# Loading the second pair ahead of theta's weight, with the first batch's orders rewritten on every engine

## The chip, the cores and the metric

The program runs on one core of one Trainium2 chip. The metric is device time of one execution in microseconds (us), lower is better. All times are medians over several executions; every execution quoted here was in the normal ("fast") state, so like is compared with like. "The clock" below is the granted TensorE clock that the profile records, as a share of full speed (1.00). In the views of the profile PE is TensorE (matrix products), PEld its weight loads, DVE VectorE, ACT ScalarE, POOL GpSimd and SPq the queue that issues transfers (DMA); L312 is line 312 of the kernel shown.

## The reference, cut to what matters

Two stages in sequence. The first is retention (linear attention with decay) over 4 batches, 8 heads, 768 steps and 64 elements a head; the second takes its output as `x` (4 x 768 x 512).

```python
# stage 1, per batch and head
state = gamma * state + outer(k[t], v[t])
y[t]  = scale * q[t] @ state
# stage 2
theta = x @ w_theta
zr, zi = x * cos(theta), x * sin(theta)
y = w_tok_r @ zr + w_tok_i @ zi          # mixes the 768 steps
u = x + y
out = u + maximum(u @ w_ch, 0)
```

Everything arrives as float32; the kernel computes its products in bfloat16.

## The kernel before

A batch is cut into three "pairs" of 256 steps (pair `n`, each with two halves of 128), so there are 12 pairs; pairs 0 to 2 are the first batch. For each pair the kernel does:

- `prep`: cast k, scale q and v by the decay (out of the float32 tile `pair`), `flip`: transpose k and q on TensorE and copy the result out of its PSUM tile (`kqT<-kq_ps` in the views, 0.69 us on VectorE);
- `ret_A` score block, `ret_mask` its mask on VectorE, `ret_S` state, `ret_Y` output within the block, `ret_I` output from the earlier state ("inter-chunk block"), `ret_out` copy to `xT`;
- `x_pe`: transpose `xT` back to `x`; `theta`: four matmuls and two sines on ScalarE; `zmul`: the two products `z` on VectorE;
- `moe_M`: the token mix, one step being two matmuls (it needs the transposed token weights, `w_flip`, and one z), then `moe_u`, `moe_U`, `moe_O`, `moe_out` and the store.

With `tc.manual_schedule()` the order of the lines in this source is the schedule of every engine at once. The first batch is a hand-written list before the main loop, cut here to the part that the argument touches:

```python
loads("p0 th p1 w0 p2 w1 w2 p3 w3 ch p4 w4 p5 w5")   # order of the DMA loads
def keep_busy(times):                                # filler, computes nothing wanted
    for _ in range(times):
        nc.tensor.matmul(warm_ps, warm[:, 0:P], warm, start=True, stop=True)
DP, PP = (DV, PL), (PL, PL)       # halves of a scaling: VectorE + GpSimd, or GpSimd alone
...                               # pair 0: prep, flips, retention
theta(0, 0); flip(1, "k"); theta(0, 1); flip(1, "q")
prep(1, "v", PP); w_cast(0); x_pe(0, None)
ret_A(1, 0); ret_mask(1, 0)
...                               # rest of pair 1
prep(2, "k", (PL,)); zmul(0, 0); flip(2, "k"); prep(2, "q", DP)
theta(1, 0); zmul(0, 1); theta(1, 1)
moe_M(0, 0, 1)
flip(2, "q"); prep(2, "v", PP); w_cast(1); w_cast(2); x_pe(1, AC.copy)
moe_M(0, 1, 2)
ret_A(2, 0); ret_mask(2, 0); ret_S(2, 0); state_out(2, 0)
ret_A(2, 1); ret_mask(2, 1); zmul(1, 0)
...
for n in range(nG, B * nG + 1):   # main loop from pair 3 on; round n starts retention of pair n
    ...
```

Of the kernel before, what the change touches and what calls it, by code (L numbers as in the profile page):

```python
# [14 lines left out]
FT = mybir.dt.float32  # L15
# [17 lines left out]
def kernel(  # L33
# [64 lines left out]
    def loads(order):  # L98
        for what in order.split():
            if what == "th":  # L100
                load_w512("th", moe_w_theta)
            elif what == "ch":
                load_w512("ch", moe_w_ch)
            elif what[0] == "w":
                for r in range(2):
                    load_wtok(r, int(what[1:]))
            else:
                for name in "kqv":
                    load(int(what[1:]), name)

    loads("p0 th p1 w0 p2 w1 w2 p3 w3 ch p4 w4 p5 w5")


    warm = const.tile([P, dm], BF)
# [72 lines left out]
            copy(t, ps)  # L187
        st[n, name + "T"], st[n, name + "_ps"] = t, ps

    def flip_out(n, name):  # L190
        nc.vector.tensor_copy(st[n, name + "T"], st[n, name + "_ps"])

    def flip_dma(n, name):
        t = work.tile([P, 2, NP, P], BF, name="kqT", bufs=6)
# [112 lines left out]
             st[n, "x_ps"].rearrange("p a j e -> p a (j e)"))  # L307

    def theta(n, a):
        th_ps = psum.tile([P, dm], FT, name="th_ps", tag="acc", bufs=2)  # L310
        for j in range(NP):
            nc.tensor.matmul(th_ps, st[n, "xT"][:, a, j, :], wth[:, j, :], start=(j == 0),  # L312
                             stop=(j == NP - 1))
        cs = work.tile([P, 2, dm], BF, name="cs", bufs=3)
        nc.scalar.activation(cs[:, 0, :], th_ps, AF.Sin, bias=halfpi, scale=1.0)  # L315
        nc.scalar.activation(cs[:, 1, :], th_ps, AF.Sin, bias=zerob, scale=1.0)  # L316
        st[n, "cs", a] = cs
# [53 lines left out]

    def moe_out(m):
        b, t0 = divmod(m, nT)
        ot = work.tile([P, dm], FT, name="ot", bufs=8)
        nc.vector.scalar_tensor_tensor(ot, mo[m]["o"], 0.0, mo[m]["u"], ALU.max, ALU.add)  # L375
        mo[m]["ot"] = ot

# [3 lines left out]

    wrow = {}

    def w_cast(t0):
        for r in range(2):
            row = work.tile([P, S], BF, name="wrow", bufs=5)
            nc.gpsimd.tensor_copy(row, wdma[r, t0])  # L387
            wrow[r, t0] = row

    def w_flip(r, t0, copy=True):  # L390
# [71 lines left out]
    def keep_busy(times):  # L462
        for _ in range(times):
            nc.tensor.matmul(warm_ps, warm[:, 0:P], warm, start=True, stop=True)
# [10 lines left out]
    flip(0, "q")  # L475
    keep_busy(2)
    prep(0, "v", PP)
    nc.gpsimd.tensor_copy(wth, wdma["th"])
    ret_A(0, 0)
    ret_mask(0, 0)  # L480
    keep_busy(2)
    ret_S(0, 0)
    state_out(0, 0)
    ret_A(0, 1)
    ret_mask(0, 1)
    ret_Y(0, 0)
    keep_busy(1)
    ret_S(0, 1)
    ret_I(0, 1)
    state_out(0, 1)  # L490
    prep(1, "k", (AC,))
    keep_busy(1)
    ret_Y(0, 1)
    ret_out(0, 0, DV.tensor_copy)
    ret_out(0, 1, DV.tensor_copy)
    keep_busy(3)
    prep(1, "q", DP)
    theta(0, 0)
    flip(1, "k")
    theta(0, 1)  # L500
    flip(1, "q")
    prep(1, "v", PP)
    w_cast(0)
    x_pe(0, None)
    ret_A(1, 0)
    ret_mask(1, 0)
    x_out(0, DV.tensor_copy)
    keep_busy(3)
    ret_S(1, 0)
    state_out(1, 0)  # L510
    ret_A(1, 1)
    ret_mask(1, 1)
    ret_Y(1, 0)
    ret_I(1, 0)
    w_flip(0, 0)
    ret_S(1, 1)
    state_out(1, 1)
    ret_I(1, 1)
    ret_Y(1, 1)
    ret_out(1, 0, AC.copy)  # L520
    ret_out(1, 1, DV.tensor_copy)
    w_flip(1, 0)
    prep(2, "k", (PL,))
    zmul(0, 0)
    flip(2, "k")
    prep(2, "q", DP)
    theta(1, 0)
    zmul(0, 1)
    theta(1, 1)
    moe_M(0, 0, 1)  # L530
    flip(2, "q")
    prep(2, "v", PP)
    w_cast(1)
    w_cast(2)
    x_pe(1, AC.copy)
    moe_M(0, 1, 2)
    ret_A(2, 0)
    ret_mask(2, 0)
    ret_S(2, 0)
    state_out(2, 0)  # L540
    ret_A(2, 1)
    ret_mask(2, 1)
    zmul(1, 0)
    ret_Y(2, 0)
    ret_I(2, 0)
    ret_I(2, 1)
    w_flip(0, 1, False)
    w_flip(1, 1, False)
    ret_Y(2, 1)
    ret_out(2, 0, AC.copy)  # L550
    ret_out(2, 1, DV.tensor_copy)
    w_out(0, 1)
    w_out(1, 1)
    zmul(1, 1)
    prep(3, "k", (PL,))
    moe_M(0, 2, 3)
    theta(2, 0)
    flip(3, "k")
    prep(3, "q", DP)
    theta(2, 1)  # L560
    moe_M(0, 3, 4)
    x_pe(2)
    w_flip(0, 2, False)
    w_out(0, 2, AC.copy)
    moe_M(1, 0, 2)
    zmul(2, 0)
    flip(3, "q")
    prep(3, "v", PP)
    w_cast(3)
    moe_M(1, 2, 4)  # L570
    zmul(2, 1)
    moe_M(0, 4, 5)


    tiles_of = {nG - 2: [], nG - 1: [0, 1]}
# [16 lines left out]
    for n in range(nG, B * nG + 1):  # L592
        mine, done = tiles_of[n], tiles_of[n - 1]
        late, two = n > nG, len(mine) > 1
        nxt = n + 1 in pairs

        if nxt and n + 1 >= K_DMA:
            flip_dma(n + 1, "k")
        if nxt and n + 1 >= Q_DMA:
            flip_dma(n + 1, "q")  # L600
        if n <= X_DMA and n + 3 in pairs:
            load(n + 3, "k")
        if n >= U_DMA:
            moe_U_dma(done[1])
        def preps(engines):
            prep(n + 1, "q", engines)
            prep(n + 1, "v", PP)
            if n in (nG, nG + 1):
                w_cast(n - nG + 4)

        if n == nG:
            nc.gpsimd.tensor_copy(wch, wdma["ch"])
        if nG + 3 < n + 1 < Q_DMA:
            preps(PP)
        if late:
            ret_I(n - 1, 1)

        if n in pairs:
            ret_A(n, 0)
            ret_mask(n, 0)  # L620
        if n == nG:
            moe_M(0, 5, nT)
            w_flip(1, 2)
            moe_u(0)
            moe_M(1, 4, nT)
            moe_u(1)
        if late:
            ret_Y(n - 1, 1)
            ret_S(n - 1, 1)
            ret_out(n - 1, 0, nc.scalar.copy)  # L630
            ret_out(n - 1, 1, nc.scalar.copy)
            state_out(n - 1, 1)
            if n < nG + 3:
                prep(n + 1, "k", (PL,))
                if n > nG + 1:
                    preps(DP)
            if n - 1 >= X_DMA:
                x_dma(n - 1)
        if n > X_DMA and n + 3 in pairs:
            load(n + 3, "k")  # L640
        if n + 3 in pairs:
            load(n + 3, "q")

        first = mine[0]
        moe_M(first, 0, 3 if two else 2)
        if late:
            theta(n - 1, 0)
            if n - 1 < X_DMA:
                x_pe(n - 1)
            if n == nG + 1:  # L650
                preps(DP)
            theta(n - 1, 1)
        if two:
            moe_M(first, 3, nT)
            moe_u(first)
        for name, limit in (("k", K_DMA), ("q", Q_DMA)):
            if nxt and nG + 1 < n + 1 < limit and (n > nG + 1 or name == "k"):
                flip(n + 1, name)
        if n + 1 >= K_DMA and not two:
            moe_M(first, 2, 4)  # L660
        if n + 3 in pairs:
            load(n + 3, "v")
        for t in stores_in(n):
            store(t)
        if n + 1 >= U_DMA:
            moe_U_dma(first)

        if n in pairs:
            ret_S(n, 0)
            state_out(n, 0)  # L670
            ret_A(n, 1)
            ret_mask(n, 1)
            ret_Y(n, 0)
            ret_I(n, 0)
        if n < U_DMA:
            moe_U(done)
        if n == nG:
            prep(n + 1, "k", (AC,))
            preps(DP)
        if n == nG or n + 1 < K_DMA and not two:  # L680
            moe_M(first, 2, 4)
        early_z = late and n < nG + 3
        if early_z and n > nG + 1:
            zmul(n - 1, 0)
        if n < nG + 3:
            w_tok(n - nG + 3)
        if early_z:
            zmul(n - 1, 0 if n == nG + 1 else 1)
        if not two:
            moe_M(first, 4, nT)  # L690
            if n == nG + 1:
                flip(n + 1, "q")
            moe_u(first)
            if n == nG + 1:
                zmul(n - 1, 1)
        elif n in pairs:
            moe_M(mine[1], 0, nT)
        if n + 2 in pairs and n > nG + 1:
            prep(n + 2, "k", (AC,))
        if n + 2 in pairs and n + 2 >= Q_DMA:  # L700
            prep(n + 2, "q", PP)
            prep(n + 2, "v", PP)
        if two and n in pairs:
            moe_u(mine[1])
        for i, t in enumerate(done):
            if n == nG:
                flip(n + 1, "kq"[i])
            moe_O(t)
            moe_out(t)
        if late and not early_z:  # L710
            zmul(n - 1, 0)
            zmul(n - 1, 1)
        if n not in pairs:
            moe_M(mine[1], 0, nT)
            moe_u(mine[1])
# [43 lines left out]
```

## Time and profile before

| what | value |
|---|---|
| median of 3 executions | 168.18 us (167.8 to 168.19) |
| TensorE busy, whole span | 93% of 166.5 us |
| granted clock | 1.00 throughout |
| first score block of pairs 0, 1, 2 | 9.90, 18.34, 27.38 us |
| theta of pair 2 begins | 32.15 us |
| inter-chunk block of pair 3 begins | 48.41 us |
| theta of pair 5 begins | 70.61 us |

The last rows are landmarks read from TensorE's timeline. The next view gives the busy time of the engines in three stretches of 10 us of the kernel before; after the stretch and its length come TensorE, weight loads, VectorE, ScalarE and GpSimd (count of instructions in brackets), then the granted clock, the DMA share and GB/s.

```profile
10.00:20.00 10.00, 8.54 (x171) 5.33 (x174) 6.93 (x9) 5.07 (x10) 7.19 (x6) 1.00 1.15 319
20.00:30.00 10.00, 8.57 (x189) 6.08 (x190) 8.69 (x12) 6.90 (x13) 7.78 (x9) 1.00 1.12 332
30.00:40.00 10.00, 9.38 (x111) 5.97 (x111) 8.86 (x13) 5.01 (x8) 7.65 (x7) 1.00 1.03 316
```

TensorE and VectorE are both close to full from 20 to 40 us: 8.57 and 9.38 us of each 10 on TensorE, 8.69 and 8.86 on VectorE.

### The profile page before, as it was taken

To read this page: it belongs to the slowest core of one execution; us is meant where nothing else is said; L and a number is where in the kernel's file an instruction comes from. 1 tells how busy PE (TensorE), PEld (TensorE's weight loads), DVE (VectorE), ACT (ScalarE), POOL (GpSimd) and SP (SyncE) were. 2 spreads that over 40 slices of the span, in tenths; PEclk is the share of its full clock that TensorE was granted. 3 is DMA by queue.
4 is the path that set the end of the run, shared out by engine and by line. 5 is a ranking of instruction groups with operands and counts; after the bars stand their busy time and mean duration, and the time that the engine had idled before them with its cause. 6 is when DMAs were issued, how large, how long until landed. Compare 5 with 4: busy or idle time off the path is not lost.

```text
span 166.5 us, 4614 instructions
## 1 busy us (share of the span) xinstructions
PE 155.2 (93%) x1933; PEld 87.2 (52%) x1959; DVE 102.4 (61%) x137; ACT 79.1 (48%) x137; POOL 66.6 (40%) x82
## 2 busy tenths in 40 slices
PE   6969897899999999999999999999999999999991
PEld 2345664664755667555555554455545444444460
DVE  2257798878686699939446464584554736334442
ACT  7216568371819467687847827447083350000010
POOL 6275959786685877771442703600000000000000
PEclk9999999999999999999999999999999999999999
DMA  4999999999999999999999999998996161753343
GB/s 122 309 345 307 326 326 354 286 328 317 293 311 349 277 278 331 309 202 250 206 231 298 163 242 203 195 233 168 266 145 185 32 189 32 231 115 100 106 141 135
DMA packets 68901, 38.45 MB, mean 231 GB/s; under 512 B 26256, under 2 KB 63376, under 8 KB 68880
## 3 DMA queue, kind: packets, MB, share of 16 engines
q1 hardware_dynamic: 68736, 38.02, 90.2%
q8 instruction: 15, 0.25, 0.7%
q10 hardware_dynamic: 144, 0.13, 0.2%
q14 instruction: 6, 0.05, 0.1%
HBM read 25.69 MB, written 6.29 MB: 192 GB/s over the span
## 4 chain that ended last, share of the span: by engine, by line
PE 77%; DVE 12%; DMA 3%; issue 3%; ACT 1%; POOL 1%; DVEq 0%; SPq 0%; POOLq 0%
PE y_ps L340 33%; PE o_ps L368 12%; PE th_ps L312 11%; PE at_ps L208 4%; PE yT_ps L231 4%; DVE at L215 4%; DMA pair<-in_q_dram 3%; PE yT_ps L245 3%; PE st_ps L262 3%; PE kq_ps L183 3%; DVE z L322 2%; PE w_ps L393 2%; DVE kqT L187 2%; PE y_ps L420 2%; DVE kqb L175 1%
## 5 line engine op out<-in xcount | busy, mean ns | idle before, releaser
L340 PE MATMUL y_ps<-z,wtr 128*128 128x512 bf16 x133 | 50.5, 379 | 1.1
L340 PE MATMUL y_ps<-z,wti 128*128 128x512 bf16 x122 | 46.2, 379 | 0.4 <-issue 0.2
L347 DVE TENSOR_TENSOR u<-y_ps,x_sb 128x512 bf16<-128x512 f32 x23 | 15.9, 690 | 27.0 <-PE y_ps L340 27.0
L215 DVE TENSOR_TENSOR at<-at_ps,maskp 128x1024 bf16<-128x1024 f32 x24 | 29.3, 1221 | 4.6 <-PE at_ps L208 4.6
L175 POOL TENSOR_TENSOR kqb<-pair,qscp 128x512 bf16<-128x512 f32 x17 | 19.3, 1150 | 28.9 <-DMA pair<-in_q_dram 26.0
L175 POOL TENSOR_TENSOR kqb<-pair,vscp 128x512 bf16<-128x512 f32 x24 | 26.6, 1131 | 5.0 <-DMA pair<-in_v_dram 4.9
L285 ACT CAST xT<-yT_ps 128x512 bf16<-128x512 f32 x20 | 13.5, 739 | 30.0 <-PE yT_ps L231 29.9
L375 DVE SCALAR_TENSOR_TENSOR ot<-o_ps,u 128x512 f32<-128x512 f32 x23 | 15.9, 690 | 13.2 <-PE o_ps L368 13.2
L312 PE MATMUL th_ps<-wth,xT 128*128 128x512 bf16 x93 | 23.2, 379 | 0.5 <-ACT xT L285 0.3
L368 PE MATMUL o_ps<-wch,uT 128*128 128x512 bf16 x92 | 22.8, 379 | 0.3
L340 PEld LDWEIGHTS <-wtr 128*128 128x128 bf16 x138 | 13.5, 98 | 13.8
L276 ACT CAST stbd<-st_ps 64x256 bf16<-64x256 f32 x40 | 14.7, 368 | 12.5 <-PE st_ps L262 12.0
L340 PEld LDWEIGHTS <-wti 128*128 128x128 bf16 x138 | 13.5, 98 | 13.6 <-ACT wti L400 0.4
L315 ACT ACTIVATE cs<-th_ps,halfpi 128x512 bf16<-128x512 f32 x24 | 16.5, 689 | 7.0 <-PE th_ps L312 6.6
L322 DVE TENSOR_TENSOR z<-cs,x_sb 128x1024 bf16<-128x1024 bf16 x24 | 18.8, 808 | 0.1
L316 ACT ACTIVATE cs<-th_ps,zerob 128x512 bf16<-128x512 f32 x24 | 16.5, 687 | 0.0
L312 PEld LDWEIGHTS <-xT 128*128 128x128 bf16 x96 | 8.9, 98 | 11.0 <-ACT xT L285 1.0
L368 PEld LDWEIGHTS <-uT 128*128 128x128 bf16 x92 | 8.8, 98 | 10.5 <-issue 0.6
L208 PE MATMUL at_ps<-kqT 64*64 64x128 bf16 x384 | 10.6, 221 | 2.6 <-DVE at L215 1.8
L430 ACT COPY uT<-u_ps 128x384 bf16<-128x384 bf16 (+1 forms) x2 | 0.7, 372 | 25.5 <-PE u_ps L429 25.5
L187 DVE COPY kqT<-kq_ps 128x1024 bf16<-128x1024 bf16 x14 | 9.6, 688 | 4.2 <-PE kq_ps L183 4.1
L387 POOL CAST wrow<-wtok 128x768 bf16<-128x768 f32 x12 | 10.5, 902 | 0.3 <-DMA wtok<-in_moe_w_tok_i_dram 0.2
(61 smaller groups left out, 164.4 us busy)
## 6 DMA issues: line engine op xcount, KB each, us to landing
pair<-in_k_dram SPq DMA_DIRECT2D x12, 512.0 KB, 6.7
pair<-in_q_dram SPq DMA_DIRECT2D x12, 512.0 KB, 7.7
pair<-in_v_dram SPq DMA_DIRECT2D x12, 512.0 KB, 8.2
out_dram<-ot SPq DMA_DIRECT2D x23, 256.0 KB, 2.6
wtok<-in_moe_w_tok_r_dram SPq DMA_DIRECT2D x6, 384.0 KB, 6.4
wtok<-in_moe_w_tok_i_dram SPq DMA_DIRECT2D x6, 384.0 KB, 5.8
w<-in_moe_w_theta_dram SPq DMA_DIRECT2D x1, 1024.0 KB, 8.3
w<-in_moe_w_ch_dram SPq DMA_DIRECT2D x1, 1024.0 KB, 8.5
```

Of the source, the lines that this page charges most:

```text
L175: engines[two].tensor_mul(dst[:, two], src[:, two], _bcast_last(sc[:, 2 * g + two], D))
L208: nc.tensor.matmul(at_ps[half, par, j, :], kT[rows, two, j, half], qT[rows, :, j, half], start=(j == 0), stop=(j == NP - 1), skip_group_ch ...
L215: nc.vector.tensor_mul(at.rearrange("p a j t -> p (a j) t"), at_ps.rearrange("p a j t -> p (a j) t"), _bcast_mid(maskp[:, two].rearrange(" ...
L276: nc.scalar.copy(stbd[(c + 1) % 2][sl, :, sl], st_ps[b][sl])
L312: nc.tensor.matmul(th_ps, st[n, "xT"][:, a, j, :], wth[:, j, :], start=(j == 0), stop=(j == NP - 1))
L315: nc.scalar.activation(cs[:, 0, :], th_ps, AF.Sin, bias=halfpi, scale=1.0)
L316: nc.scalar.activation(cs[:, 1, :], th_ps, AF.Sin, bias=zerob, scale=1.0)
L322: nc.vector.tensor_mul(zs[b][:, c], st[n, "cs", a], _bcast_mid(xs[b][:, c, :], 2))
L340: nc.tensor.matmul(y_ps, wT[r][:, s0, t0 * P:(t0 + 1) * P], zs[b][:, s0, r, :], start=(s0 == 0 and r == 0), stop=(s0 == nT - 1 and r == 1))
L347: nc.vector.tensor_add(u, mo[m]["y"], xs[b][:, t0, :])
L368: nc.tensor.matmul(o_ps, mo[m]["uT"][:, j, :], wch[:, j, :], start=(j == 0), stop=(j == nD - 1))
L375: nc.vector.scalar_tensor_tensor(ot, mo[m]["o"], 0.0, mo[m]["u"], ALU.max, ALU.add)
```

## The change

The intent: have q, k and v of the second pair at hand about 3 us sooner, so that the retention of two pairs runs without holes first and their thetas follow once theta's weight has come. For that the first batch's order is rewritten on all engines, three fillers go (27 to 24), the first rounds of the loop are rearranged, and the output tile gets 5 buffers for 8. The diff, cut to its core (lines that were only moved away are mostly left out):

```diff
-    loads("p0 th p1 w0 p2 w1 w2 p3 w3 ch p4 w4 p5 w5")
+    loads("p0 p1 th w0 p2 w1 w2 p3 w3 ch p4 w4 p5 w5")
...
-        cs = work.tile([P, 2, dm], BF, name="cs", bufs=3)
+        cs = work.tile([P, 2, dm], BF, name="cs", bufs=4)
...
-        ot = work.tile([P, dm], FT, name="ot", bufs=8)
+        ot = work.tile([P, dm], FT, name="ot", bufs=5)
...
-    theta(0, 0)
-    flip(1, "k")
-    theta(0, 1)
     flip(1, "q")
     prep(1, "v", PP)
-    w_cast(0)
-    x_pe(0, None)
+    for a in range(2):
+        nc.gpsimd.tensor_copy(wth[:, 2 * a:2 * a + 2], wdma["th"][:, 2 * a:2 * a + 2])
+    keep_busy(2)
     ret_A(1, 0)
     ret_mask(1, 0)
...
+    theta_mm(0, 0, "y")
     ret_Y(1, 1)
     ret_out(1, 0, AC.copy)
     ret_out(1, 1, DV.tensor_copy)
+    sines(0, 0)
+    w_cast(0)
+    x_pe(1)
+    theta(0, 1)
+    zmul(0, 0)
+    theta(1, 0)
+    w_flip(0, 0, False)
+    w_flip(1, 0, False)
+    w_out(0, 0)
+    w_out(1, 0, DV.tensor_copy)
+    theta(1, 1)
     prep(2, "k", (PL,))
+    zmul(0, 1)
+    moe_M(0, 0, 1)
+    flip(2, "k", None)
     prep(2, "q", DP)
+    moe_M(0, 1, 2)
+    flip_out(2, "k")
     flip(2, "q")
     prep(2, "v", PP)
+    zmul(1, 0)
+    moe_M(0, 2, 3)
     ret_A(2, 0)
     ret_mask(2, 0)
...                 # (rest of the first batch, and in the loop, round of pair 3:)
         if n == nG:
             prep(n + 1, "k", (AC,))
-            preps(DP)
+            moe_M(first, 3, nT)
+            moe_u(first)
+            w_tok(n - nG + 3)
...
-            if n == nG:
-                flip(n + 1, "kq"[i])
+            if n == nG and i == 1:
+                flip(n + 1, "k", nc.scalar.copy)
+                preps(DP)
+                flip(n + 1, "q")
             moe_O(t)
             moe_out(t)
+        if n == nG:
+            moe_M(first + 1, 0, 2)
```

More of the change, by code (lines that the diff above doesn't have):

```diff
@@ L188, in flip, with flip_out @@
         st[n, name + "T"], st[n, name + "_ps"] = t, ps
-    def flip_out(n, name):
-        nc.vector.tensor_copy(st[n, name + "T"], st[n, name + "_ps"])
+    def flip_out(n, name, copy=nc.vector.tensor_copy):
+        copy(st[n, name + "T"], st[n, name + "_ps"])
     def flip_dma(n, name):
@@ L309, in theta, with theta_mm @@
     def theta(n, a):
-        th_ps = psum.tile([P, dm], FT, name="th_ps", tag="acc", bufs=2)
+        theta_mm(n, a)
+        sines(n, a)
+    def theta_mm(n, a, tag="acc"):
+        th_ps = psum.tile([P, dm], FT, name="th_ps" if tag == "acc" else "y_ps", tag=tag,
+                          bufs=2 if tag == "acc" else 1)
         for j in range(NP):
@@ L313, in theta, with sines @@
                              stop=(j == NP - 1))
-        cs = work.tile([P, 2, dm], BF, name="cs", bufs=3)
+        st[n, "th", a] = th_ps
+    def sines(n, a):
+        th_ps = st[n, "th", a]
+        cs = work.tile([P, 2, dm], BF, name="cs", bufs=4)
         nc.scalar.activation(cs[:, 0, :], th_ps, AF.Sin, bias=halfpi, scale=1.0)
@@ L382, with w_cast @@
     wrow = {}
-    def w_cast(t0):
+    def w_cast(t0, copy=nc.gpsimd.tensor_copy):
         for r in range(2):
             row = work.tile([P, S], BF, name="wrow", bufs=5)
-            nc.gpsimd.tensor_copy(row, wdma[r, t0])
+            copy(row, wdma[r, t0])
             wrow[r, t0] = row
@@ L477 @@
     prep(0, "v", PP)
-    nc.gpsimd.tensor_copy(wth, wdma["th"])
     ret_A(0, 0)
@@ L481 @@
     keep_busy(2)
+    prep(1, "k", (AC,))
     ret_S(0, 0)
@@ L486 @@
     ret_Y(0, 0)
-    keep_busy(1)
+    flip(1, "k", AC.copy)
+    prep(1, "q", DP)
     ret_S(0, 1)
@@ L490 @@
     state_out(0, 1)
-    prep(1, "k", (AC,))
     keep_busy(1)
     ret_Y(0, 1)
-    ret_out(0, 0, DV.tensor_copy)
+    ret_out(0, 0, AC.copy)
     ret_out(0, 1, DV.tensor_copy)
-    keep_busy(3)
-    prep(1, "q", DP)
-    theta(0, 0)
-    flip(1, "k")
-    theta(0, 1)
+    keep_busy(1)
     flip(1, "q")
     prep(1, "v", PP)
-    w_cast(0)
-    x_pe(0, None)
+    for a in range(2):
+        nc.gpsimd.tensor_copy(wth[:, 2 * a:2 * a + 2], wdma["th"][:, 2 * a:2 * a + 2])
+    keep_busy(2)
     ret_A(1, 0)
     ret_mask(1, 0)
-    x_out(0, DV.tensor_copy)
-    keep_busy(3)
+    x_pe(0, None)
+    keep_busy(1)
     ret_S(1, 0)
     state_out(1, 0)
+    x_out(0, AC.copy)
     ret_A(1, 1)
@@ L514 @@
     ret_I(1, 0)
-    w_flip(0, 0)
     ret_S(1, 1)
@@ L521 @@
     ret_out(1, 1, DV.tensor_copy)
-    w_flip(1, 0)
+    sines(0, 0)
[9 more added lines that the diff above has]
+    theta(1, 1)
     prep(2, "k", (PL,))
-    zmul(0, 0)
-    flip(2, "k")
+    zmul(0, 1)
+    moe_M(0, 0, 1)
+    flip(2, "k", None)
     prep(2, "q", DP)
-    theta(1, 0)
-    zmul(0, 1)
-    theta(1, 1)
-    moe_M(0, 0, 1)
+    moe_M(0, 1, 2)
+    flip_out(2, "k")
     flip(2, "q")
     prep(2, "v", PP)
-    w_cast(1)
-    w_cast(2)
-    x_pe(1, AC.copy)
-    moe_M(0, 1, 2)
+    zmul(1, 0)
+    moe_M(0, 2, 3)
     ret_A(2, 0)
@@ L541 @@
     ret_A(2, 1)
+    zmul(1, 1)
     ret_mask(2, 1)
-    zmul(1, 0)
     ret_Y(2, 0)
@@ L546 @@
     ret_I(2, 1)
-    w_flip(0, 1, False)
-    w_flip(1, 1, False)
+    w_cast(1)
+    moe_M(0, 3, 4)
     ret_Y(2, 1)
-    ret_out(2, 0, AC.copy)
-    ret_out(2, 1, DV.tensor_copy)
-    w_out(0, 1)
-    w_out(1, 1)
-    zmul(1, 1)
-    prep(3, "k", (PL,))
-    moe_M(0, 2, 3)
-    theta(2, 0)
-    flip(3, "k")
-    prep(3, "q", DP)
-    theta(2, 1)
-    moe_M(0, 3, 4)
-    x_pe(2)
-    w_flip(0, 2, False)
-    w_out(0, 2, AC.copy)
+    ret_out(2, 0, DV.tensor_copy)
+    ret_out(2, 1, AC.copy)
+    w_flip(0, 1)
+    w_flip(1, 1)
+    theta(2, 0)
+    theta(2, 1)
+    x_pe(2)
+    prep(3, "k", (PL,))
     moe_M(1, 0, 2)
     zmul(2, 0)
+    flip(3, "k")
+    prep(3, "q", PP)
+    moe_M(1, 2, 4)
+    zmul(2, 1)
+    w_cast(2, AC.copy)
+    moe_M(0, 4, nT)
     flip(3, "q")
     prep(3, "v", PP)
-    w_cast(3)
-    moe_M(1, 2, 4)
-    zmul(2, 1)
-    moe_M(0, 4, 5)
+    moe_u(0)
+    moe_M(1, 4, nT)
+    w_flip(0, 2)
+    w_flip(1, 2)
+    moe_u(1)
     tiles_of = {nG - 2: [], nG - 1: [0, 1]}
@@ L611 @@
         if n == nG:
+            w_cast(n - nG + 3)
             nc.gpsimd.tensor_copy(wch, wdma["ch"])
@@ L620 @@
             ret_mask(n, 0)
-        if n == nG:
-            moe_M(0, 5, nT)
-            w_flip(1, 2)
-            moe_u(0)
-            moe_M(1, 4, nT)
-            moe_u(1)
         if late:
@@ L644 @@
         first = mine[0]
-        moe_M(first, 0, 3 if two else 2)
+        if n == nG + 1:
+            moe_M(first, 2, 4)
+        else:
+            moe_M(first, 0, 3 if two or n == nG else 2)
         if late:
@@ L678 @@
             prep(n + 1, "k", (AC,))
-            preps(DP)
-        if n == nG or n + 1 < K_DMA and not two:
+            moe_M(first, 3, nT)
+            moe_u(first)
+            w_tok(n - nG + 3)
+        elif n == nG + 2:
             moe_M(first, 2, 4)
@@ L684 @@
             zmul(n - 1, 0)
-        if n < nG + 3:
+        if nG < n < nG + 3:
             w_tok(n - nG + 3)
@@ L688 @@
             zmul(n - 1, 0 if n == nG + 1 else 1)
-        if not two:
+        if late and not two:
             moe_M(first, 4, nT)
@@ L695 @@
                 zmul(n - 1, 1)
-        elif n in pairs:
+        elif two and n in pairs:
             moe_M(mine[1], 0, nT)
@@ L705 @@
         for i, t in enumerate(done):
-            if n == nG:
-                flip(n + 1, "kq"[i])
+            if n == nG and i == 1:
+                flip(n + 1, "k", nc.scalar.copy)
+                preps(DP)
+                flip(n + 1, "q")
             moe_O(t)
             moe_out(t)
+        if n == nG:
+            moe_M(first + 1, 0, 2)
         if late and not early_z:
```

## The prediction

> **What bounds the kernel now.** I read the page from the top (busy time, slices), then the chain that ended last, then the timelines of TensorE, VectorE and GpSimd up to 50 us, because the change rewrites only that stretch.
>
> ```profile
> PE 155.2 (93%) x1933; PEld 87.2 (52%) x1959; DVE 102.4 (61%) x137; ACT 79.1 (48%) x137; POOL 66.6 (40%) x82
> ...
> PE   6969897899999999999999999999999999999991
> ...
> DMA  4999999999999999999999999998996161753343
> ...
> PE 77%; DVE 12%; DMA 3%; issue 3%; ACT 1%; POOL 1%; DVEq 0%; SPq 0%; POOLq 0%
> ```
>
> The reader is to see that TensorE is the bound: full from slice 9 (about 33 us) to the end, 77% of the chain. A slice is 4.16 us; only the first eight have holes, and DMA is full there too, so early on TensorE waits for data and for small chains through the other engines. Only those holes can be won. The timeline of TensorE shows them (start, duration, what):
>
> ```profile
> 9.90 0.42 PE L208 MATMUL at_ps<-kqT 64*64 64x128 bf16 x16 [0.35 <-DVE kqT L187]
> ...
> 13.88 0.82 PE L464 MATMUL y_ps<-warm 128*128 128x512 bf16 x3
> 14.77 1.04 PE L312 MATMUL th_ps<-wth,xT 128*128 128x512 bf16 x4
> ...
> 18.34 0.42 PE L208 MATMUL at_ps<-kqT 64*64 64x128 bf16 x16 [0.34 <-DVE kqT L187]
> 18.69 0.82 PE L464 MATMUL y_ps<-warm 128*128 128x512 bf16 x3
> ...
> 27.38 0.42 PE L208 MATMUL at_ps<-kqT 64*64 64x128 bf16 x16
> ...
> 29.12 0.42 PE L208 MATMUL at_ps<-kqT 64*64 64x128 bf16 x16 [1.07 <-DVE at L215]
> ...
> 32.15 1.04 PE L312 MATMUL th_ps<-wth,xT 128*128 128x512 bf16 x4 [0.32 <-ACT xT L285]
> ```
>
> These are retention of pair 0 (9.90), theta of pair 0 (14.77), retention of pairs 1 (18.34) and 2 (27.38), theta of pair 2 (32.15). L464 is filler (keep_busy) that computes nothing wanted. Issue-to-issue steps of the same timeline give the real work: four 128x512 matmuls 0.865 us, eight 128x128 transposes 0.45, six 0.335, a score block (L208) 0.3, a state block (L262) 0.3, an output block (L231) 0.36, an inter-chunk block (L245) 0.22, one step of the token mix (two matmuls) 0.43.
>
> Between 9.90 and 32.15 (22.25 us) the real work is: 4 flips of k and q 1.8, 2 of x 0.9, 4 of token weights 1.34, 4 thetas 3.46, 3 mix steps 1.3, 6 score blocks 1.8, 5 state 1.5, 6 output 2.15, 5 inter-chunk 1.1: 15.35 us. So 6.9 us are lost, of which 10 fillers are 2.16. From 32.15 to 48.41, where the inter-chunk block of pair 3 begins, the same sum gives about 15.3 us of 16.26: 1 us lost. In each of the next two loop rounds (48.41, 58.63, 68.83) about 0.5 us is lost. All that this change could win is a part of some 9 us.
>
> The second limit is the arrival of data, seen on GpSimd:
>
> ```profile
> 8.83 2.04 POOL L175 TENSOR_TENSOR kqb<-pair,vscp 128x512 bf16<-128x512 f32 x2 [0.16 <-DMA pair<-in_v_dram]
> 11.59 1.89 POOL L478 CAST wth<-w 128x2048 bf16<-128x2048 f32 x1 [0.71 <-DMA w<-in_moe_w_theta_dram]
> 15.24 1.55 POOL L175 TENSOR_TENSOR kqb<-pair,qscp 128x512 bf16<-128x512 f32 x1 [1.76 <-DMA pair<-in_q_dram]
> ...
> 23.67 1.04 POOL L175 TENSOR_TENSOR kqb<-pair,qscp 128x512 bf16<-128x512 f32 x1 [0.77 <-DMA pair<-in_q_dram]
> 25.14 2.49 POOL L175 TENSOR_TENSOR kqb<-pair,vscp 128x512 bf16<-128x512 f32 x2 [0.42 <-DMA pair<-in_v_dram]
> ```
>
> v of pair 0 is there at 8.8, theta's weight at 11.6, q of pair 1 at 15.2, q of pair 2 at 23.7 us.
>
> [...] at 29.12 TensorE idles 1.07 us behind one masked block, though other work follows in its order. So here every order is a bet on arrival times. [...] the product z (L322) takes 0.67 us at 23.14 with GpSimd idle, 1.54 at 25.19 beside the v scaling of 25.14:
>
> ```profile
> 23.14 0.67 DVE L322 TENSOR_TENSOR z<-cs,x_sb 128x1024 bf16<-128x1024 bf16 x1
> 23.73 0.68 DVE L187 COPY kqT<-kq_ps 128x1024 bf16<-128x1024 bf16 x1
> 24.33 0.93 DVE L175 TENSOR_TENSOR kqb<-pair,qscp 128x512 bf16<-128x512 f32 x1
> 25.19 1.54 DVE L322 TENSOR_TENSOR z<-cs,x_sb 128x1024 bf16<-128x1024 bf16 x1
> 26.65 0.68 DVE L187 COPY kqT<-kq_ps 128x1024 bf16<-128x1024 bf16 x1
> ```
>
> **The change, part by part.**
>
> Loads. Pair 1 (1.57 MB) goes ahead of theta's weight (1.05 MB). The bytes up to both are the same, so from the first token weights on nothing arrives sooner or later. From the 1.7 us of one k, q or v: k of pair 1 at about 10.4, q 12.2, v 14.0, theta's weight 16.7 us. Pair 1 is about 3 us earlier, theta's weight 5 us later.
>
> 9.9 to 20 us. ScalarE casts k of pair 1 at 10.4 to 11.5 and copies its flip (1.0 us) at 13.0; VectorE scales half of q at 13.5 to 14.1 and evacuates one block to 14.8; the q flip on TensorE is at 14.2, its copy 14.8 to 15.5. So pair 1's first score block is at 15.5, not 18.34: 2.8 us won. Then the chain score, mask (1.24), score, mask runs to 18.9. Theta's weight is cast in halves by GpSimd at 16.7 to 18.6, so theta of the first half of pair 0 lies at 18.6 to 19.5, just as the last mask is ready; the last output block ends at 19.9 against 22.4 before. But before had by then both thetas of pair 0 and one weight flip (2.07 us of work), and here one theta (0.87). Of 2.5 us won 1.2 are owed: 1.3 net.
>
> 20 to 33 us. The next flip of x needs the xT evacuation of ScalarE (20.0 to 20.7): 0.8 us of TensorE idle, gone from the 1.3. From there VectorE leads. It has, in its order: x copy, z, two token-weight copies (one of them ScalarE's before), z, q scaling, two flip copies, z. At 0.6 us each for copies and scaling, 0.47 for the weight copies, 0.6 for a free z and 1.5 for one that meets GpSimd (casting k at 21.9, scaling q at 23.7, v from 25.1; I take two of three as meeting), this is 4 x 0.6 + 2 x 0.47 + 0.8 + 2 x 1.5 = 7.1 us from 21.2: 28.3. The third mix step waits for that last z and stands ahead of pair 2's first score block, which so starts at about 28.3 to 28.7 instead of 27.38. Score, mask, z, mask, evacuation put theta of pair 2 at about 32.9 instead of 32.15, with one mix step (0.43) more done: 0.3 us behind, or level.
>
> 33 to 50 us. The order takes mix steps of both first tiles and both flips ahead of the loop, the third token-weight cast goes from GpSimd to ScalarE, and two mix steps of the fourth tile (0.86) are drawn into the first round. Work up to the inter-chunk block of pair 3: 15.7 us against 15.3, with 0.86 more done. Here I see one new wait: the q flip of pair 4 stands right after its k flip and needs VectorE's scaling, which is behind the evacuation of the first output: 0.6 + 0.6 us, less 0.45 of the k flip, about 0.7. On the other side the old waits here (1 us) may go.
>
> Three fillers fewer (27 to 24) take 0.65 us of TensorE time, but only where no wait replaces them; they are in the sums above. Output tiles with 5 buffers for 8: tile 8 reuses the buffer of tile 3, whose store is issued at 107.23 us and lands 2.6 us later, while its evacuation stood at 108.07. That is about 1.5 us on VectorE, which is 55% busy there, and the next block that needs it (mask of pair 10's second score block) has more slack. I count 0.
>
> Sum of my walk: 0 to +1 us. A walk by hand finds every wait that an error of 0.3 us makes, and an order that was tuned on traces has fewer; I take off about 1.2 us. That is a choice, not a reading. Prediction: 167.6 us, 0.6 below the median of 168.18.
>
> **Rivals.** (1) VectorE becomes the bound of 20 to 33 us: already 8.7 and 8.9 of each 10 us there. For it: the sums above, each z beside GpSimd. Against it: three evacuations go to ScalarE, two come back. It would make 169 to 170. (2) The order works as meant and the early hole closes: with theta and x of both pairs at hand at 20 us, TensorE's free work (4.5 us, then pair 2) runs without a hole to theta of pair 2 at about 31 us with one mix step more: 1.6 us, with the round after it 2.5: 165.7. (3) The gain is hidden by arrival: pair 2 comes no sooner than 23.67, so a win before it turns into a wait for it: 168. (4) Fewer output buffers stall the tail: 168.5 to 169.5.
>
> **Range and chances.** 2% is 3.4 us, half of all the loss before 32 us; even rival 2 does not reach it: 0.06. Slower by 2% needs VectorE to hold up TensorE by 3.4 us net: 0.03. Within: 0.91. Range 165.7 to 169.4.
>
> **What would show it.** Right: pair 1's first score block near 15.5; theta's cast waiting for DMA at 16.7; TensorE waiting for ScalarE's evacuation near 20; pair 2's first score block behind 27.4 with a wait on z; from 75 us the same sequence as before, shifted by one constant. Wrong: score blocks of pair 2 near 26 us, or z never beside GpSimd (rival 2); waits above 1 us after 107 us (rival 4); pair 1 not earlier (then the loads are not served in order).

## The result, and the profile after

The changed kernel takes 176.55 us (175.84 to 176.88, four executions) where the kernel before takes 168.19 (167.8 to 168.29, four executions). The ratio is 1.0496 (95% interval 1.046 to 1.0532): 8.3 us slower by the means. Ratios here are the mean time of one kernel's fast runs over that of the other's of the same rounds, so not quite the ratio of the quoted medians.

The page of the kernel after shows where to look: busy time, TensorE's 40 slices with the granted clock in the same slices, and the chain's shares. A slice is 4.38 us here.

```profile
PE 156.7 (89%) x1928; PEld 88.0 (50%) x1956; DVE 102.0 (58%) x135; ACT 81.7 (47%) x140; POOL 65.0 (37%) x82
...
PE   7878694787986989999999999999999999999991
...
PEclk9999998589999999999999999999999999999999
...
PE 72%; DVE 9%; DMA 5%; SPq 4%; issue 3%; ACT 2%; POOL 1%; DVEq 0%
```

TensorE is as busy as before in microseconds (156.7 for 155.2) in a longer span, with a deep hole in the seventh slice (26.3 to 30.7 us, the 4) and lesser ones up to the fifteenth. From the seventh slice on the clock row reads 8, 5, 8. That did not occur before, and nothing in the prediction spoke of it. The chain has 5% of theta's weight in it (9.58 us from issue to landing), which invites the story that the late weight is the loss. An experiment below tests that.

The timeline of TensorE after (start, duration, what, and in brackets the idle time before it with what ended it), cut to the landmarks and the large waits:

```profile
15.53 0.42 PE L208 MATMUL at_ps<-kqT 64*64 64x128 bf16 x16 [0.35 <-DVE kqT L187]
...
20.18 0.59 PE L317 MATMUL y_ps<-wth,xT 128*128 128x512 bf16 x2 [0.61 <-POOL wth L509]
...
28.37 0.62 PE L183 MATMUL kq_ps<-ident,kqb 128*128 128x128 bf16 x8 [0.86 <-DVE kqb L175]
30.37 0.59 PE L349 MATMUL y_ps<-z,wtr 128*128 128x512 bf16 x1 [1.38 <-DVE z L331]
...
31.31 0.64 PE L208 MATMUL at_ps<-kqT 64*64 64x128 bf16 x16
...
55.31 0.62 PE L183 MATMUL kq_ps<-ident,kqb 128*128 128x128 bf16 x8 [1.57 <-DVE kqb L175]
57.49 0.39 PE L245 MATMUL yT_ps<-kqT,stbd 128*128 128x128 bf16 x4
```

Pair 1's first score block is at 15.53 us, 2.8 sooner than before. Pair 2's, which was at 27.38, is now at 31.31. It stands behind two waits for VectorE, 0.86 for the q scaling and 1.38 for a z. And it takes 0.64 us, at a granted clock of 0.50, for the same sixteen matmuls that took 0.42 at 15.53, at 1.00: this is what half the clock looks like on one line.

The same stretch on VectorE and, below it, on GpSimd:

```profile
25.60 1.26 DVE L331 TENSOR_TENSOR z<-cs,x_sb 128x1024 bf16<-128x1024 bf16 x1
26.79 1.52 DVE L175 TENSOR_TENSOR kqb<-pair,qscp 128x512 bf16<-128x512 f32 x1
28.23 0.68 DVE L191 COPY kqT<-kq_ps 128x1024 bf16<-128x1024 bf16 x1
...
29.63 0.68 DVE L331 TENSOR_TENSOR z<-cs,x_sb 128x1024 bf16<-128x1024 bf16 x1
```

```profile
18.11 2.02 POOL L509 CAST wth<-w 128x1024 bf16<-128x1024 f32 x2 [2.00 <-DMA w<-in_moe_w_theta_dram]
...
25.27 2.49 POOL L175 TENSOR_TENSOR kqb<-pair,vscp 128x512 bf16<-128x512 f32 x2 [0.48 <-DMA pair<-in_v_dram]
```

VectorE works almost without a pause, but in the wrong order for TensorE: q of pair 2, at hand since 23.66 us (when GpSimd begins to scale its half), is scaled at 26.79 only, behind two weight copies and a z, and takes 1.52 us beside GpSimd's scaling of v (25.27 to 27.76); the same scaling of pair 1 took 0.68 at 13.20, nearly all of it with GpSimd idle. The z for which TensorE stands is the last of the row.

Last, two windows of the kernel after: the 3.4 us before the slow clock, and the 6.8 us of it (columns as above).

```profile
26.20:29.60 3.40, 1.71 (x19) 0.98 (x17) 3.29 (x4) 0.93 (x2) 3.40 (x4) 1.00 0.92 296
29.60:36.40 6.80, 4.77 (x87) 3.19 (x91) 3.76 (x5) 0.73 (x2) 3.89 (x5) 0.50 1.08 330
```

TensorE worked half of the first window; in the second the clock was 0.50 throughout, and 1.00 again behind it. In the kernel before, the first window held 2.19 us of TensorE work and the clock stayed at 1.00. The four executions of the kernel after had a mean clock of 0.981, 0.979, 0.99 and 0.99 over their whole length: if all of the loss is time at 0.50, as in this trace, 0.02 of 175 us is 7 us of it and 0.01 is 3.5 us (an estimate from these means). No wait of TensorE around the slow stretch was above 1.38 us. That the little work of the first window brought the slow clock is a theory so far; e1 below tests it.

How far the kernel after lags behind the one before, landmark by landmark (from the two timelines of TensorE):

| landmark | before | after | lag |
|---|---|---|---|
| first score block of pair 1 | 18.34 | 15.53 | -2.8 |
| first score block of pair 2 | 27.38 | 31.31 | 3.9 |
| theta of pair 2 | 32.15 | 37.52 | 5.4 |
| inter-chunk block of pair 3 | 48.41 | 57.49 | 9.1 |
| theta of pair 5 | 70.61 | 79.29 | 8.7 |
| theta at the same place, late in the loop | 111.18 | 119.85 | 8.7 |

At theta of pair 2 the kernel after has done one mix step more (0.43 us), at the inter-chunk block of pair 3 two more (0.86), so the lag in work is 4.9 there and 8.2 here. From 70 us on it is constant: the rest of the program, with its five output buffers, runs as before.

### The profile page after: what moved, and what is told of

It is laid out like the page before. It is cut to its first block, busy times and chain, and to the rows that moved or that the text cites. A ratio compares the mean times of both kernels' runs of the same rounds, so it can differ in the third digit from the quotient of the medians.

```text
span 175.2 us, 4603 instructions
## 1 busy us (share of the span) xinstructions
PE 156.7 (89%) x1928; PEld 88.0 (50%) x1956; DVE 102.0 (58%) x135; ACT 81.7 (47%) x140; POOL 65.0 (37%) x82
## 4 chain that ended last, share of the span: by engine, by line
PE 72%; DVE 9%; DMA 5%; SPq 4%; issue 3%; ACT 2%; POOL 1%; DVEq 0%
PE y_ps L349 32%; PE o_ps L377 11%; PE th_ps L317 10%; DMA w<-in_moe_w_theta_dram 5%; SPq L81 4%; PE yT_ps L231 3%; PE at_ps L208 3%; PE yT_ps L245 3%; DVE z L331 2%; PE st_ps L262 2%; DVE kqb L175 2%; PE kq_ps L183 2%; PE y_ps L429 1%; DVE at L215 1%; PE w_ps L402 1%
## 5 line engine op out<-in xcount | busy, mean ns | idle before, releaser
L349 PE MATMUL y_ps<-z,wti 128*128 128x512 bf16 x123 | 46.9, 381 | 0.7 <-ACT wti L409 0.2
L356 DVE TENSOR_TENSOR u<-y_ps,x_sb 128x512 bf16<-128x512 f32 x23 | 15.9, 690 | 26.8 <-PE y_ps L349 26.8
L285 ACT CAST xT<-yT_ps 128x512 bf16<-128x512 f32 x21 | 14.2, 736 | 32.0 <-PE yT_ps L231 32.0
L317 PE MATMUL th_ps<-wth,xT 128*128 128x512 bf16 x90 | 21.9, 379 | 0.1
L324 ACT ACTIVATE cs<-th_ps,halfpi 128x512 bf16<-128x512 f32 x23 | 15.8, 688 | 5.9 <-PE th_ps L317 5.5
L325 ACT ACTIVATE cs<-th_ps,zerob 128x512 bf16<-128x512 f32 x23 | 15.8, 687 | 0.0
L183 PE MATMUL kq_ps<-ident,kqb 128*128 128x128 bf16 x120 | 9.4, 219 | 3.5 <-DVE kqb L175 2.7
L231 PE MATMUL yT_ps<-at,kqb 64*64 64x128 bf16 x384 | 11.0, 224 | 1.0 <-issue 0.6
```

The source lines that it names most:

```text
L231: nc.tensor.matmul(yT[a][par * D:(par + 1) * D, j, :], vp[half, two, h * D:(h + 1) * D], at[half, par, j, :], start=(two == 0 and j == 0), ...
L317: nc.tensor.matmul(th_ps, st[n, "xT"][:, a, j, :], wth[:, j, :], start=(j == 0), stop=(j == NP - 1))
L324: nc.scalar.activation(cs[:, 0, :], th_ps, AF.Sin, bias=halfpi, scale=1.0)
L325: nc.scalar.activation(cs[:, 1, :], th_ps, AF.Sin, bias=zerob, scale=1.0)
L349: nc.tensor.matmul(y_ps, wT[r][:, s0, t0 * P:(t0 + 1) * P], zs[b][:, s0, r, :], start=(s0 == 0 and r == 0), stop=(s0 == nT - 1 and r == 1))
L356: nc.vector.tensor_add(u, mo[m]["y"], xs[b][:, t0, :])
```

## The experiments

The prediction's sum had missed 9 us, so the runs were to share them out. The theories: **the clock** (waits leave TensorE too little work, and half a clock follows); **the orders** (VectorE's order around pair 2 and the loop's new order make the waits); **the late weight** (theta's weight comes later, and everything behind it too). Each run was beside the kernel before on the same chip; its medians there were 168.41 (e1 to e4), 168.29 (e5 to e8), 168.48 (e9 to e12) and 167.9 (e13, e14). All runs have four executions, and all computed the right result except e10.

**e1_fill: fillers in the two waits.** The kernel after with eight fillers where TensorE waited.

```diff
     moe_M(0, 1, 2)
+    fill(3)                 # as keep_busy, but into the bank of the score blocks
     flip_out(2, "k")
     flip(2, "q")
     prep(2, "v", PP)
     zmul(1, 0)
+    fill(5)
     moe_M(0, 2, 3)
```

> The changed kernel with eight filler matmuls (into the score bank, which is free then) in TensorE's two waits between 27 and 30.4 us, nothing else. Theory 'clock': the half clock that follows these waits (29.8 to 36.2 us in the profile) is what the change lost most by; with it gone the granted clock is 1.00 and the time falls by about 3 us, to 173.5. Theory 'chain': the waits on VectorE set the pace and the half clock mostly stretches work that lies beside them; the clock is 1.00, the time falls by at most 1.5 us, to 175 or above.

173.73 us (172.98 to 174.27), ratio 1.0321 (1.0276 to 1.0367). The two windows of e1:

```profile
26.20:29.60 3.40, 3.19 (x27) 1.72 (x25) 3.29 (x5) 1.12 (x2) 3.40 (x4) 1.00 0.96 318
29.60:36.40 6.80, 5.00 (x109) 3.27 (x109) 4.79 (x7) 2.26 (x4) 4.40 (x6) 1.00 1.13 335
```

With eight useless matmuls, 0.216 us each, the window of 3.4 us holds 3.19 us of work, the clock stays at 1.00, and the kernel is 176.55 - 173.73 = 2.8 us faster, by adding work. Pair 2's first score block is at 30.83 all the same (31.31 without fillers), for VectorE is no faster. So the clock is 2.8 of the 8.3 us, and 5.5 us have another cause.

**e2_open_before and e3_open_after: which half of the change costs.** Both kernels are cut at theta of pair 2. e2 has the load order and first part ("opening") of before and the rest of after; e3 the reverse. Steps of the token mix (and one weight cast) were moved so that each is done once.

```diff
 # e2, against the kernel after
-    loads("p0 p1 th ...")  + its opening up to theta(2, 0)
+    loads("p0 th p1 ...")  + the opening of before up to theta(2, 0)
-    w_cast(2, AC.copy)
-    moe_M(0, 4, nT)
+    moe_M(0, 2, nT)
 # e3: the opening of after, then the kernel before from theta(2, 0) on
```

> Load order and opening (all up to theta of pair 2) of the kernel before, then the rest as changed. The lag against before is 4.9 us at theta of pair 2 and 8.2 us at the inter-chunk block of pair 3. Theory 'two losses': the later part loses its own 3.3 us whatever the opening does: about 171.5. Theory 'one loss': the later waits only follow from the late opening: 168 to 169.

> Load order and opening as changed, then the rest as before. Theory 'two losses': about 173 (168.2 and the 4.9 us of the opening). Theory 'one loss' read the other way, that the new order after the opening is at fault: 168 to 170. If it is slower than the changed kernel, the new rest was made for the new opening and helps it.

e2: 170.51 us (170.21 to 171.17), ratio 1.0125 (1.0086 to 1.0164), 2.1 us over the kernel before. e3: 172.91 (172.55 to 173.76), ratio 1.0269 (1.0227 to 1.0311), 4.5 us over. There are two losses, the opening's 4.5 and the later part's 2.1; together 6.6 of 8.3, so 1.7 us come only when both are there. e3's mean clock is 0.98 to 0.99, so its 4.5 us contain a share of the clock. In its trace the clock is 0.50 for 3.4 us (32.12 to 35.53), half as long as in the kernel after, so a part of the 1.7 may be the clock; no run tests that.

**e4_before_loads: the new load order alone.** The kernel before with only `"p0 p1 th ..."`.

> The kernel before with the new load order alone. Theory 'order needed': theta of pair 0 waits on TensorE for its weight (cast whole, ready near 20 us instead of 13.5) with pair 1's retention behind it: 171 to 174. Theory 'loads harmless': the loads' order costs little by itself: under 170.

175.29 us (174.27 to 175.93), ratio 1.0398 (1.0349 to 1.0447): 6.9 us slower, more than I had thought. TensorE's line:

```profile
19.82 1.86 PE L312 MATMUL th_ps<-wth,xT 128*128 128x512 bf16 x4 [5.31 <-POOL wth L478]
```

Theta of pair 0 stands in TensorE's order ahead of pair 1's flip, so all that had come early waited 5.31 us behind a weight that had not come, and four matmuls took 1.86 us at a clock of 0.50 (20 to 22 us), where the kernel before took 1.04 at 1.00. Here the new load order without a new order of work is a loss.

**e9_loads_back: the new orders with the old load order.** e1 with `"p0 th p1 ..."`.

> As e1_fill (173.7 us), with the load order of the kernel before under the new orders of the engines. Theory 'late weight': what the new order loses beside the clock comes from theta's weight arriving at 18 instead of 11.6 us; with it back early, pair 1 is 3 us later (first score block near 18.4), and the two cancel: 173 to 175. Theory 'orders': the orders alone lose it, and the new load order was a gain: 176 or more. If under 172, the new load order was a loss even under the orders written for it.

176.87 us (175.91 to 177.32), ratio 1.0494 (1.0442 to 1.0545), against 173.73 for e1: going back costs 3.1 us. The k flip of pair 1 waits 2.08 us, its first score block comes at 18.60, and the clock falls to 0.59 between 16 and 20 us, which is part of the 3.1 (how much no run isolates). So under the new orders the new load order is a gain, and the loss must lie in the orders.

Little work in 3.4 us did not bring a slow clock every time: from 32.0 to 35.4 us e9 has 1.31 us of TensorE work, less than the 1.71 of the kernel after, and the clock is 1.00 there and up to 40. How much work is enough is not shown.

**e10_weight_at_hand: theta's weight never late.** e1, with the cast of the weight made from k of pair 1, which has long been there. Its output is wrong, which doesn't matter for the time. The work is the same.

```diff
-        nc.gpsimd.tensor_copy(wth[:, 2 * a:2 * a + 2], wdma["th"][:, 2 * a:2 * a + 2])
+        nc.gpsimd.tensor_copy(wth[:, 2 * a:2 * a + 2], <raw k of pair 1>)
```

> As e1_fill, but theta's weight is cast from k of pair 1, which is there at 10.4 us (wrong results on purpose; the weight is still loaded at its place). GpSimd then casts it right after v of pair 1, by about 18.2 instead of 20.2 us. Theory 'late weight': all that follows starts 1 to 2 us earlier, score block of pair 2 at 29.5 instead of 30.8: 172 or below. Theory 'arrival of pair 2 and VectorE': the earlier thetas only wait longer: within 0.5 us of e1_fill.

173.5 us (173.04 to 173.89), ratio 1.0295 (1.0261 to 1.0328): 0.2 us below e1, within the spread. Two lines of e10's TensorE, then two of its VectorE, and last the z of e1:

```profile
19.47 1.03 PE L317 MATMUL y_ps<-wth,xT 128*128 128x512 bf16 x3
...
30.88 0.42 PE L208 MATMUL at_ps<-kqT 64*64 64x128 bf16 x16
```

```profile
25.32 1.53 DVE L331 TENSOR_TENSOR z<-cs,x_sb 128x1024 bf16<-128x1024 bf16 x1
26.78 1.53 DVE L175 TENSOR_TENSOR kqb<-pair,qscp 128x512 bf16<-128x512 f32 x1
```

```profile
25.80 1.01 DVE L331 TENSOR_TENSOR z<-cs,x_sb 128x1024 bf16<-128x1024 bf16 x1
```

The wait for the weight is gone (no bracket at 19.47), and pair 2's score block is at 30.88, where e1 has it at 30.83. The 0.5 us won were lost again in the z at 25.32: it fell beside GpSimd's v scaling, which waited 0.56 us for v (it begins at 25.26 here), and took 1.53 us where e1's, begun at 25.80, took 1.01. Both ended at about 26.8. Each of the two took longer beside the other here: in e10 the z before it, at 22.93 and nearly all of it with GpSimd idle, took 0.68 us, and the v scaling took 2.49 where that of pair 1, at 14.18 and beside copies on VectorE, took 2.04. The q scaling took 1.53 in both runs and ended at about 28.3. So z and q scaling ended at the same times in e10 and e1, although the z began 0.48 us apart; v's scaling began at 25.26 and 25.21. That v's arrival sets these ends is my reading of the two traces. Under these orders the late weight is refuted as a cause, although the chain of waits names it.

**e5_mix_behind and e6_q_on_gpsimd: two repairs of the waits.** Both are e1 with one move: e5 puts the third mix step behind pair 2's first score and state block; e6 gives both halves of q's scaling to GpSimd.

```diff
 # e5
-    moe_M(0, 2, 3)
     ret_A(2, 0); ret_mask(2, 0); ret_S(2, 0); state_out(2, 0)
+    moe_M(0, 2, 3)
 # e6
-    prep(2, "q", DP)
+    prep(2, "q", PP)
```

> As e1_fill (173.7 us), with the third mix step of the first tile put behind pair 2's first score and state block instead of ahead of it, so that TensorE does not wait there for VectorE's product z. Theory 'place of the wait': the score block starts when the q flip's copy is done, about 29.8 instead of 30.8 us, and the whole rest with it: 172.7. Theory 'absorbed': the next wait (mask, 1.08 us) takes the gain: within 0.3 us of e1_fill.

> As e1_fill, with q of pair 2 scaled by GpSimd alone. VectorE's half takes 1.52 us there beside GpSimd, at the end of its chain. Theory 'VectorE sets the pace': its chain is 1.5 us shorter, GpSimd needs 1 us longer for q but was waiting 0.5 for v: score block near 29.5, time about 172.5. Theory 'arrival sets it': GpSimd is late instead, v of pair 2 and the second token weights come 1 us later: time within 0.5 us of e1_fill.

e5: 172.55 us (172.51 to 174.19), ratio 1.0272 (1.0209 to 1.0336). e6: 173.01 (172.72 to 173.39), ratio 1.027 (1.0229 to 1.0312). That is 1.2 and 0.7 below e1's median, but the ranges overlap. Theta of pair 2 moved from 35.60 to 35.18 and 34.85. By these landmarks each helps a little; neither is the cause by itself.

**e7_all_repairs and e8_old_open_repaired: the loop's waits.** e7 has both moves and two repairs in the loop's first round: token weights flipped ahead of `moe_u`, and q of pair 4 scaled by GpSimd alone. e8 is e2 with the two loop repairs.

> As e1_fill with the repairs of e5 and e6 and two more in the first loop round: q of pair 4 scaled by GpSimd alone, and the fourth token weights' flips ahead of the addition u on VectorE (the changed kernel waits 0.6 us for such a copy and 0.9 to 1.6 us for that scaling). If the losses of opening and round add up: 173.7 less 2 less 1.6, about 170. What is left above 168.4 is then the price of the late theta weight. If they are absorbed: 171.5 or more.

> As e2_open_before (load order and opening of before, the changed rest; 170.5 us), with the two repairs of the loop round of e7. If the two waits in that round (0.58 and 1.06 us) are what the changed rest costs: 168.9. Below 168.0 it would beat the kernel before, since it does two mix steps of the next tile early. If 170 or more, the loss of the rest lies elsewhere.

e7: 171.66 us (170.98 to 172.46), ratio 1.019 (1.0142 to 1.0237): 2.1 below e1, where 3.6 were expected if the losses add up, so about 1.5 was absorbed. e8: 170.35 (169.27 to 170.81), ratio 1.0101 (1.0052 to 1.015), no different from e2's 170.51. That is a miss: I had pointed at the waits of 0.58 and 1.06 us in e2's first round and taken both away. Between theta of pair 2 and the inter-chunk block of pair 3, TensorE's waits of 0.18, 0.58 and 1.06 us became five of 0.16 to 0.37, 1.37 us in all, and the stretch took 18.9 us instead of 19.0. Here a wait removed was for the most part split up; that VectorE was late anyway is my reading, not shown.

**e11_old_loop: e2 with the loop of before.** So only the stretch between theta of pair 2 and the loop is new.

> As e2_open_before (170.5 us), with the first loop rounds' order of the kernel before; only the order between theta of pair 2 and the loop stays as changed. Theory 'rounds': the changed rounds (two flips between the outputs, mix steps of the next tile drawn ahead) cost the 2.1 us: 168.4, and less than 168.0 would beat before. Theory 'stretch before the loop': no change, 170.5.

169.04 us (169.0 to 169.37), ratio 1.0035 (1.0006 to 1.0064). Against e2 this is 1.5 us less: the rearranged rounds cost 1.5 us, the stretch before them 0.6, so it fits neither theory alone. The landmarks agree: theta of pair 5 is at 72.62 in e2, 71.21 in e11, 70.61 before.

**e12_new_open_repaired, e13_pair2_first and e14_q_early: the opening's order on VectorE.** e12 is e3 (new loads and opening, old rest) with both moves and five fillers. e13 rewrites e12's order from 22 to 33 us so that pair 2 goes first: q's half right behind the first z, flip copies and mask ahead of the other z, one weight copy on ScalarE, mix steps behind the score blocks. It has none of the five fillers, and q is again halved between VectorE and GpSimd. e14 is e12 with the q scaling alone brought forward, halved in the same way (GpSimd's cast of k moves with it).

```diff
 # e13, against e12 (cut)
+    prep(2, "k", (PL,))
     theta(1, 0)
     zmul(0, 0)
+    flip(2, "k", None)
+    prep(2, "q", DP)
+    flip_out(2, "k")
     theta(1, 1)
...
+    ret_A(2, 0)
+    ret_mask(2, 0)
     w_flip(1, 0, False)
-    w_out(1, 0, DV.tensor_copy)
+    w_out(1, 0, AC.copy)
...
     zmul(0, 1)
...
     ret_I(2, 1)
+    moe_M(0, 0, 2)
+    zmul(1, 0)
```

> New load order and opening, with the repairs of e5 and e6 and fillers in one wait, then the rest as before: the best I can make of the new load order. From e3_open_after (172.9 us): the clock should stay at 1.00 (1 us or so) and the score block of pair 2 should start at about 29.0 instead of 30.95. If the opening's loss is these waits and the clock: 169.5 to 170.5. If it reaches 168.3 the new load order costs nothing by itself; above 171 something else in the opening is slower.

> As e12_new_open_repaired (170.8 us; score block of pair 2 at 28.5, theta of pair 2 at 33.8 us), with VectorE's and TensorE's order of 22 to 33 us rewritten: the q half, both flip copies and the mask of pair 2 go ahead of the products z and the token-weight copies (one goes to ScalarE), the mix steps come after the score blocks. Theory 'order on VectorE': the score block comes near 27 us, theta of pair 2 near 31.8: 168 to 169. Theory 'new load order': pair 2 cannot start sooner because the thetas of pairs 0 and 1 fall into its time: 170.5 or more.

> As e12_new_open_repaired, with only the q scaling of pair 2 back on VectorE and GpSimd in halves, but on VectorE right after the first z (24 us) and not after the weight copies and the second z. Theory 'order on VectorE': the q flip comes about 1 us sooner, yet its copy stands behind the two weight copies, z and the k copy, so that the score block gains little: 28.0 us, time 170.3. Theory 'new load order': no change.

| run | us (range) | ratio (interval) | score block, pair 2 | inter-chunk, pair 3 |
|---|---|---|---|---|
| e3 | 172.91 (172.55 to 173.76) | 1.0269 (1.0227 to 1.0311) | 30.95 | 53.07 |
| e12 | 170.82 (169.79 to 171.83) | 1.0136 (1.0084 to 1.0189) | 28.51 | 51.05 |
| e14 | 170.28 (169.48 to 171.14) | 1.013 (1.007 to 1.019) | 29.21 | 50.31 |
| e13 | 169.5 (169.26 to 169.61) | 1.0085 (1.0031 to 1.0138) | 27.44 | 49.30 |

Three lines of e13, one of TensorE and two of VectorE:

```profile
27.44 0.42 PE L208 MATMUL at_ps<-kqT 64*64 64x128 bf16 x16 [0.78 <-DVE kqT L187]
```

```profile
23.87 1.53 DVE L175 TENSOR_TENSOR kqb<-pair,qscp 128x512 bf16<-128x512 f32 x1
...
26.70 0.69 DVE L187 COPY kqT<-kq_ps 128x1024 bf16<-128x1024 bf16 x1 [0.70 <-PE kq_ps L183]
```

In e13 the same scaling takes as long (1.53 us), but 2.9 us sooner, and pair 2's score block is back at 27.44, level with the 27.38 of before. VectorE even waits 0.70 us for TensorE. So VectorE could have fed pair 2 in time; the order of its work kept it from that. It is not free: at 27.44 e13 has done two mix steps (0.86 us) and one weight flip (0.34) fewer than the kernel before, and its theta of pair 2 comes at 33.04, where 31.8 was expected and before has 32.15. Its clock stayed at 1.00 without any of the five fillers. Fillers and both moves take e3's excess from 4.5 to 2.3 us (170.82, just above the 169.5 to 170.5 expected), e13's order to 1.4 (interval 0.5 to 2.3, from the ratio; 169.5 us lies between its two theories). The intervals of e12 and e13 overlap, so the step between them rests on the landmarks of two traces more than on the times; bringing q forward alone (e14) shows no clear change.

No version beats the kernel before.

## Why the prediction was wrong

I predicted 167.6 us with 165.7 to 169.4 and gave "slower by over 2%" 3 chances in 100. It came to 176.55.

**Right, and small: the arrivals and pair 1.** k, q and v of pair 1 were expected at 10.4, 12.2 and 14.0 us and used at 10.42, 12.27 and 14.06; pair 1's first score block at 15.5 came at 15.53; TensorE's wait of 0.8 for ScalarE's evacuation, put near 20, was 0.82 and came at 21.1. Theta's weight, put at 16.7, landed 1.4 us later: the estimate counted bytes in order of issue, and the weight landed at 18.06, 9.58 us after its issue at 8.47. Why it was late no run shows. By e10 its lateness cost about 0.2 us, which is within the spread.

**The step that failed first: "20 to 33 us", the sum of VectorE.** I named the right engine (rival 1) and the right wait, a mix step that needs z in front of pair 2's score block, but put its end at 28.3 and "0.3 us behind, or level" at theta of pair 2. The last z ended at 30.31, the score block came at 31.31, theta at 37.52. Three terms were too small. The start: VectorE's x copy began at 22.60, not 21.2, since pair 1's output block ended at 21.1, not 19.9 (with the weight at hand, in e10, the copy began at 22.32). The q scaling: 0.8 us taken, 1.52 measured, for it fell beside GpSimd (0.68 in pair 1, nearly all with GpSimd idle), as only the z were allowed to in my sum. And idle time: 0.77 us for the weight flip on TensorE was not in the sum at all. A fourth term was too large, and hid about 1 us of this by luck: the three z were put at 3.6 us, two of them beside GpSimd, and took 2.62, for only one met it. So the start made 1.4 of the 2.0 us by which the last z was late, and the sum itself (7.7 us for 7.1) the rest. From there to theta of pair 2 the walk took 4.6 us; it was 7.2, and 5.3 in e1 at full clock. e10 shows why care ahead of this point does not help, e13 that another order does.

**The term that was missing altogether: the clock.** I had read a clock of 1.00 from the page and charged a wait at its own length. The waits around 28 us (one of 0.86 us and the first 0.6 of one of 1.38 before all) left TensorE 1.71 us of work in 3.4, and cost a further 2.8 us by the clock of 0.50 behind them (e1). It also changes what fillers are: I had booked the three removed as TensorE time, 0.65 us, to be had where no wait replaces them. But eight of them held the clock at 1.00 in e1, where it was 0.50 for 6.8 us without, and the new order has none where its longest gap is.

**The loop.** One new wait of 0.7 us and "the old waits here (1 us) may go": a gain on balance. The changed rounds cost 1.5 us and the stretch before them 0.6 (e2, e11). The wait that I had named was there (the q flip of pair 4, at 55.31) and took 1.57; e8 shows that removing it gains nothing clear. I read this as the queue on VectorE, not the one wait, being what holds TensorE; no run isolates it.

**The choice at the end.** "... an order that was tuned on traces has fewer; I take off about 1.2 us." It went the wrong way: the walk's 0 to +1 us was already too low.

**Rivals.** Rival 1 in kind, at 169 to 170, was what came, and its size was short by 6.5 us. Rival 2 (all works as meant) did not come. Rival 3 (gain hidden by arrival) came in part, for q of pair 2 was there at 23.66 as before and e10's 0.5 us were lost in the z beside the scaling of v (1.53 us for 1.01); but it explains no loss. Rival 4 (output buffers) is refuted by the constant lag from 70 us to the end; all that is left of it is one wait of 0.54 us of VectorE for a store, at 117.10. As said there, from about 75 us the sequence is that of before.

**The account.** Of 8.3 us: the clock 2.8 (e1); the rearranged loop rounds 1.5 and the stretch before them 0.6 (e2, e11). That leaves 3.4 us for the waits of the opening at full clock. e13 recovers all but 1.4 (0.5 to 2.3) of the opening's loss by order alone (one weight copy goes to ScalarE). The 1.2 us of work put off in e13 could be that last 1.4; it stays open. These figures come from different kernels and need not add: e2 and e3 sum to 6.6 only.

## What to carry to other kernels

A wait on TensorE can cost more than its length: here 2.8 us more, by a clock of 0.50 for 6.8 us behind a stretch of several waits. Add up TensorE's work in such a stretch (1.71 us of 3.4 here, 3.19 with the fillers that kept 1.00; the limit is not shown), read the clock behind it, and do not take fillers for waste. When a load is moved ahead, rewrite what each engine does around the *next* arrival too; here the early pair gained 2.8 us and pair 2 lost 3.9, because VectorE had other things in hand when it came. And a chain of waits names candidates only: the late weight that it showed cost next to nothing, as one run with the weight at hand told.
